# Linear attention with decay and a gated unit: features in natural order, a block-diagonal state per head pair, r transposed pair by pair, and another order of loads

## The chip, the cores and the metric

One core of one Trainium2 chip. The metric is the device time of one execution in microseconds; a kernel's time is the median of its runs. Runs that are over 1.5% slower than the fastest of the same kernel are called slow here; ratios are taken from the other, fast runs alone. The trace has a shorter time of its own, the span from the first to the last instruction, some 2 us below the run it was taken from. The engines are PE (matmuls), DVE (VectorE), ACT (ScalarE), POOL (GpSimd) and SP, which issues the transfers. All positions in a trace are microseconds from the span's start.

## The reference, cut to what matters

Two stages. First a linear attention with a decaying state for 4 batch entries (B), 8 heads (H), 768 positions (S) and 48 features a head (D); then a gated unit on the 384 joined features.

```python
for t in range(S):
    cur = u * k[t] (outer) v[t]
    y[t] = r[t] @ (state + cur)
    state = w[:, None] * state + k[t] (outer) v[t]
x = y joined over heads                       # [B, S, 384]
gate = sigmoid(causal convolution of x, 5 taps per feature)
out = (gate * (x @ w_val)) @ w_out
```

Of the kernel before, what the change touches and what calls it, by code (L numbers as in the profile page):

```python
# [16 lines left out]
def kernel(  # L17
# [12 lines left out]
    nc = tc.nc  # L30
# [13 lines left out]
    NG = J // 2  # L44
# [3 lines left out]
    ld = ctx.enter_context(tc.tile_pool(name="ld", bufs=4))  # L48
# [40 lines left out]
    load_r(0)  # L89
    load_kv(0, "v")  # L90

# [60 lines left out]
    rs_t = ring("rs", [128, 2, NP, 2, 64], 3)  # L152
    vb_t = ring("vb", [128, U, H * 64 + 64], 4)
    dv_t = ring("dv", [128, U, H * 64 + 64], 2)
    z_t = ring("z", [128, NP * 64 + 64], 6)
# [3 lines left out]
    for t_ in rs_t:  # L159
        nc.gpsimd.memset(t_[:, :, :, :, D:64].rearrange("p c n a x -> p (c n a) x"), 0.0)  # L160
    for t_ in vb_t + dv_t:
        nc.gpsimd.memset(gaps(t_.rearrange("p c x -> p (c x)")), 0.0)
    for t_ in z_t:
        nc.vector.memset(gaps(t_), 0.0)
# [5 lines left out]



# [5 lines left out]
    def load_weights():  # L178
        nc.sync.dma_start(out=cw5, in_=moe_conv_w)
        for dst, src in ((wv_st, moe_w_val), (wo_st, moe_w_out)):  # L180
            s5 = src.rearrange("(T s par e) n -> T s par e n", T=2, s=2, par=2)
            for s in range(2):
                for par in range(2):
                    q = 2 * s + par
                    nc.sync.dma_start(  # L185
                        out=dst[32 * q : 32 * q + 32, 0:2, :],
                        in_=s5[:, s, par, 16 * s : 16 * s + 32, :].transpose([1, 0, 2]),
                    )
                    e0 = 32 * (1 - s)
                    for T in range(2):  # L190
                        p0 = 32 * (2 * T + par) + 16 * s
                        nc.sync.dma_start(  # L192
                            out=dst[p0 : p0 + 16, 2, :], in_=s5[T, s, par, e0 : e0 + 16, :]
                        )

    wvA = consts.tile([128, NT, 2, 128], BF16)
    wvB = consts.tile([128, NT, 128], BF16)
    wout = consts.tile([128, NT, DM], BF16)
    cw5p = consts.tile([KW, NT, 128], BF16)
# [3 lines left out]
    def permute_cols(eng, dA, dB, src):  # L203

        s5 = src.rearrange("p g (s par e) -> p g s par e", s=2, par=2)
        a5 = dA.rearrange("p g (s par e) -> p g s par e", s=2, par=2)
        b5 = dB.rearrange("p g (par s e) -> p g par s e", s=2, par=2)
        for s in range(2):
            eng.tensor_copy(a5[:, :, s], s5[:, :, s, :, 16 * s : 16 * s + 32])
            e0 = 32 * (1 - s)  # L210
            eng.tensor_copy(b5[:, :, :, s], s5[:, :, s, :, e0 : e0 + 16])

    def prep_conv():
        permute_cols(
            nc.vector,
            cw5p[:, 0:2, :],
            cw5p[:, 2, :].rearrange("p (g x) -> p g x", g=2),
            cw5.rearrange("p (g x) -> p g x", g=2),
        )
        cw_ps = ps_mm.tile([128, NT, 8], BF16, name="mm_ps")  # L220
        for T in range(NT):
            nc.tensor.transpose(cw_ps[:, T, 0:KW], cw5p[:, T, :], ident[0:KW, 0:KW])
        nc.vector.tensor_copy(cwT, cw_ps[:, :, 0:KW])
# [9 lines left out]
    def prep_weights():  # L233
        permute_cols(
            nc.gpsimd,
            wvA.rearrange("p k T x -> p (k T) x"),
            wvB.rearrange("p k (T x) -> p (k T) x", T=2),
            wv_st.rearrange("p k (T x) -> p (k T) x", T=2),
        )

# [3 lines left out]
    def scale_r(b, g, eng):  # L244
        rs = rs_t[(b * NG + g) % 3]
        eng.tensor_tensor(  # L246
            out=rs[:, :, :, :, 0:D].rearrange("p j n a d -> p j (n a) d"),
            in0=r_st[b].rearrange("p h (j d) -> p j h d", d=D)[:, 2 * g : 2 * g + 2],
            in1=dr.rearrange("p h j d -> p j h d")[:, 2 * g : 2 * g + 2],
            op=ALU.mult,  # L250
        )

    def transp_r(b, g):
        if g == 0:
            st["rT", b] = wk.tile([128, NP, S], BF16, name="rT", bufs=3)
        rs = rs_t[(b * NG + g) % 3]
        tr = ps_tr.tile([128, 2, NP, 128], BF16, name="tr_ps")
        for j in range(2):
            for p in range(NP):
                nc.tensor.transpose(  # L260
                    tr[:, j, p, :], rs[:, j, p].rearrange("p a x -> p (a x)"), ident
                )
        nc.scalar.copy(  # L263
            out=st["rT", b].rearrange("x n (p j) -> x j n p", j=J)[:, 2 * g : 2 * g + 2],
            in_=tr,
        )
# [51 lines left out]
    def bonus_v(n):  # L318
        for cl in range(U):
            nc.gpsimd.tensor_tensor(  # L320
                out=heads(dv_t[n % 2][:, cl], H),
                in0=v_st[n][:, cl],
                in1=st["s", n][:, cl, :, None].to_broadcast([128, H, D]),
                op=ALU.mult,
            )
# [27 lines left out]
    nz = [0]  # L353

    def state(n, cl):
# [4 lines left out]
        kv_ps = ps_kv.tile([128, NP, D], F32, name="kv_ps")  # L360
        for p in range(NP):
            for par in range(2):
                h = 2 * p + par
                nc.tensor.matmul(
                    out=kv_ps[64 * par : 64 * par + 64, p, :],
                    lhsT=ks[:, cl, p, par, :],
                    rhs=heads(vb[:, cl], H)[:, h, :],
                    start=(p == 0),
                    stop=(p == NP - 1),
                    skip_group_check=True,  # L370
                )
        if c > 0:
            for par in range(2):
                nc.tensor.matmul(
                    out=kv_ps[64 * par : 64 * par + 64],
                    lhsT=ident[:, 64 * par : 64 * par + 64],
                    rhs=heads(st["z"], NP),
                    start=False,
                    stop=True,
                    skip_group_check=True,  # L380
                )
        st["kv_ps", n, cl] = kv_ps

    def decay(n, cl):
        c = (n % NU) * U + cl
        if c == NU * U - 1:
            return
        z = z_t[nz[0] % 6]
        nz[0] += 1
        nc.vector.tensor_tensor(  # L390
            out=heads(z, NP),
            in0=st["kv_ps", n, cl],
            in1=wct[:, :, None].to_broadcast([128, NP, D]),
            op=ALU.mult,
        )
# [4 lines left out]
    def y_out(n):  # L400
# [3 lines left out]
        ys = [ps_mm.tile([128, NT, 128], F32, name="mm_ps") for cl in range(U)]  # L404
        first = set()
        for kind, cl in (("z", 0), ("z", 1), ("a", 0), ("d", 0), ("a", 1), ("d", 1)):
            z = st.get(("zin", n, cl))
            if kind == "z" and z is None:
                continue
            for T2 in range(2):  # L410
                for h in range(H):
                    par, p = h % 2, h // 2
                    T = 2 if T2 else h // 4
                    q = (2 * (h // 4) + h % 2) if T2 else h % 4
                    rows = slice(64 * par, 64 * par + D)
                    s = p % 2
                    c0 = (48 if s == 0 else 0) if T2 else 16 + 16 * s
                    if kind == "z":
                        lt = z[rows, 64 * p + c0 : 64 * p + c0 + 32]
                        rh = rT[rows, p, cl * C : cl * C + C]  # L420
                    elif kind == "a":
                        lt = vb[:, cl, 64 * h + c0 : 64 * h + c0 + 32]
                        rh = st["at", n, cl][:, par, p, :]
                    else:
                        lt = dv[:, cl, 64 * h + c0 : 64 * h + c0 + 32]
                        rh = ident
                    nc.tensor.matmul(  # L427
                        out=ys[cl][32 * q : 32 * q + 32, T, :],
                        lhsT=lt,
                        rhs=rh,  # L430
                        start=(cl, q) not in first,
                        stop=(kind == "d" and T2 == 1),
                        skip_group_check=True,
                    )
                    first.add((cl, q))
            if kind == "d":
                t0 = PAD + cu * W + cl * C
                nc.scalar.copy(out=xT_t[b % 2][:, :, t0 : t0 + C], in_=ys[cl])  # L438
# [21 lines left out]
    def value(n):  # L460
# [3 lines left out]
        for Ts in ((0, 1), (2,)):  # L464
            v_ps = ps_mm.tile([128, len(Ts), W], F32, name="mm_ps")
            for i, T in enumerate(Ts):
                for kt in range(NT):
                    nc.tensor.matmul(  # L468
                        out=v_ps[:, i, :],
                        lhsT=wvA[:, kt, T, :] if T < 2 else wvB[:, kt, :],  # L470
# [35 lines left out]
    load_kv(1, "kv")  # L506
    load_weights()
    scale_k(0)
    scale_r(0, 0, nc.vector)
    scale_r(0, 1, nc.gpsimd)  # L510
    scale_r(0, 2, nc.vector)
    cast_v(0)
    for par in range(2):
# [3 lines left out]
        )  # L517

    for i in range(N + 3):
        x, a, y, f = i, i - 1, i - 2, i - 3  # L520
        if ok(x + 2):
            load_kv(x + 2, "kv")
        if x % NU == 0 and x // NU + 1 < B:
            load_r(x // NU + 1)
        if ok(a):
            prod(a)

        rb, rg = divmod(x + NU - 1, NG)
        if ok(x):
            transp_k(x)  # L530
        if x == 0:
            transp_r(0, 0)
            transp_r(0, 1)
            transp_r(0, 2)
# [67 lines left out]
```

## The kernel before: what the change and the argument touch

Both kernels take the positions in chunks of 128. Two chunks are a unit (256 positions of one batch entry), so there are 12 units. A loop of 15 passes is a software pipeline: pass i transposes k of unit i, forms the scores of unit i-1, the y of unit i-2, and the gated unit of unit i-3. Heads stand in PE tiles in pairs, each padded from 48 to 64 rows. In these traces PE takes its instructions in the order of the program: it stood idle for 8.4 us in front of the r transposes at 100.33 us, with output matmuls behind them whose input had been ready since 90.8. So the place of a step in the pass matters.

r of a whole batch entry (three units) is loaded, scaled and transposed into `rT`, one third per pass. Its positions are interleaved six to a partition (J = 6), so the copy from PSUM has to put position p*6+j in its place:

```python
def transp_r(b, g):
    ...                                       # 8 transposes: 2 values of j, 4 head pairs
    nc.scalar.copy(
        out=st["rT", b].rearrange("x n (p j) -> x j n p", j=J)[:, 2 * g : 2 * g + 2],
        in_=tr,                               # written bf16 elements are 12 bytes apart
    )
```

The order of the loop, cut:

```python
for i in range(N + 3):
    x, a, y, f = i, i - 1, i - 2, i - 3
    load_kv(x + 2, "kv")
    if x % NU == 0 and x // NU + 1 < B:
        load_r(x // NU + 1)                   # first used further down in this same pass
    prod(a); transp_k(x); conv(f); scale_k(x + 1)
    bonus(a); attn(a, 0); mask_at(a, 0); state(a, 0); decay(a, 0); bonus_v(a)
    scale_r(x // NU + 1, x % NU, nc.gpsimd)
    cast_v(x + 1); value(f)
    attn(a, 1); mask_at(a, 1); state(a, 1); decay(a, 1)
    y_out(y)
    transp_r(x // NU + 1, x % NU)             # PE stands here if r is late
    project(f)
    ...                                       # pass 0 also prepares the weights
```

Because y leaves PE in pieces of 32 features, the features of x stood in a permuted order; the weights were loaded in 24 small pieces to match.

## Time and profile before

| | before |
|---|---|
| median at the prediction, 3 runs | 169.73 us (168.91 to 170.16) |
| span of the trace | 165.8 us |
| busy: PE, DVE, ACT, POOL | 62, 47, 56, 35% |
| DMA | 20.57 MB, 50.6% of 16 engines' time in the main queue |

No engine is busy for two thirds of the span, so the averages say nothing yet. The page's row of 40 slices (each digit is the busy share of one slice in tenths, 9 meaning 90% or more) is what to read: it shows stages with different limits. The prediction below shows the lines.

### The profile page before, as it was taken

What the parts mean: (1) busy time and instruction counts of PE and PEld (TensorE: products, weight loads), DVE (VectorE), ACT (ScalarE), POOL (GpSimd) and SP (SyncE); (2) the same over time, 40 slices, a digit from 0 to 9 for tenths busy, and PEclk for the clock granted to TensorE, in tenths of its full rate; (3) what the DMA queues carried; (4) which work ended last, traced back from release to release, by engine and by line L of the source; (5) the groups of instructions that cost most, each with busy time, mean ns of one, the idle gap of its engine ahead of it and who ended that gap; (6) DMA issues with size and microseconds to landing.
All of it is one profiled execution on the core that took longest, in us unless ns stands there. A gap on an engine that the chain in (4) does not pass through costs nothing.

```text
span 165.8 us, 4872 instructions
## 1 busy us (share of the span) xinstructions
PE 103.5 (62%) x2123; PEld 81.6 (49%) x2123; DVE 77.2 (47%) x135; ACT 92.9 (56%) x109; POOL 58.9 (35%) x85
## 2 busy tenths in 40 slices
PE   0123100023579689596969108996969999999980
PEld 0112100022378568475747105775757878777750
DVE  0549000009898362391937500391947593953220
ACT  3979950009375928849394205849395817325441
POOL 7745000064877360370903024270906061230000
PEclk9999999999999978999999855899999999999999
DMA  4998338993187600390927940281927702020222
GB/s 74 269 247 187 104 105 169 301 229 73 24 170 167 218 4 0 94 195 6 248 45 182 241 151 0 88 166 38 241 47 174 182 31 99 4 97 12 91 95 95
DMA packets 58863, 20.57 MB, mean 124 GB/s; under 512 B 50773, under 2 KB 58842, under 8 KB 58842
## 3 DMA queue, kind: packets, MB, share of 16 engines
q1 hardware_dynamic: 58714, 20.26, 50.6%
q8 instruction: 16, 0.26, 0.7%
q14 instruction: 5, 0.04, 0.1%
q0 software_dynamic: 128, 0.00, 0.1%
HBM read 15.54 MB, written 4.72 MB: 122 GB/s over the span
## 4 chain that ended last, share of the span: by engine, by line
PE 44%; SPq 17%; ACT 10%; issue 9%; DMA 7%; POOL 5%; DVE 5%; DVEq 0%; ACTq 0%; POOLq 0%
PE mm_ps L427 11%; SPq L73 7%; DMA r_st<-in_r_dram 7%; PE mm_ps L448 7%; PE mm_ps L488 7%; PE mm_ps L468 6%; ACT o_sb L495 4%; PE tr_ps L260 4%; SPq L192 4%; ACT kT L290 4%; PE at_ps L334 3%; POOL rs L246 3%; PE tr_ps L287 3%; SPq L81 3%; SPq L185 2%
## 5 line engine op out<-in xcount | busy, mean ns | idle before, releaser
L263 ACT COPY rT<-tr_ps 128x1024 bf16<-128x1024 bf16 x12 | 42.7, 3620 | 29.2 <-PE tr_ps L260 29.0
L320 POOL TENSOR_TENSOR dv<-v_st,s_sb 128x384 bf16<-128x384 f32 x24 | 19.4, 830 | 57.1 <-PE at_ps L334 56.1
L260 PE MATMUL tr_ps<-ident,rs 128*128 128x128 bf16 x96 | 10.2, 272 | 34.1 <-POOL rs L246 28.9
L346 DVE TENSOR_TENSOR at<-at_ps,mask 128x1024 bf16<-128x1024 f32 x24 | 29.3, 1221 | 2.9 <-PE at_ps L334 1.9
L246 POOL TENSOR_TENSOR rs<-r_st,dr 128x768 bf16<-128x768 f32 x10 | 18.9, 1889 | 31.3 <-DMA r_st<-in_r_dram 31.3
L438 ACT CAST xT<-mm_ps 128x384 bf16<-128x384 f32 x24 | 11.2, 479 | 32.8 <-PE mm_ps L427 32.8
L448 PE MATMUL mm_ps<-xT,cwdiag 128*128 128x256 bf16 x180 | 22.8, 274 | 7.4 <-ACT o_sb L495 7.4
L260 PEld LDWEIGHTS <-rs 128*128 128x128 bf16 x96 | 7.8, 123 | 36.2 <-POOL rs L246 29.8
L448 PEld LDWEIGHTS <-cwdiag 128*128 128x128 bf16 x180 | 17.3, 98 | 10.7 <-issue 8.2
L316 DVE COPY s_sb<-mm_ps 128x16 f32<-128x16 f32 x12 | 2.1, 173 | 41.3 <-issue 34.5
L476 DVE TENSOR_TENSOR hT<-mm_ps,gate 128x512 bf16<-128x512 f32 (+1 forms) x24 | 12.2, 552 | 9.7 <-PE mm_ps L468 9.7
L488 PE MATMUL mm_ps<-wout,hT 128*128 128x384 bf16 x72 | 14.7, 344 | 0.5 <-DVE hT L476 0.5
L287 PE MATMUL tr_ps<-ident,ks 128*128 128x128 bf16 x96 | 9.1, 250 | 7.5 <-DVE ks L269 7.5
L495 ACT COPY o_sb<-mm_ps 128x384 f32<-128x384 f32 x24 | 12.2, 536 | 2.3 <-PE mm_ps L488 1.8
L279 POOL CAST vb<-v_st 128x384 bf16<-128x384 f32 x24 | 13.1, 576 | 0.0
L290 ACT COPY kT<-tr_ps 128x1024 bf16<-128x1024 bf16 x12 | 12.7, 1060 | 0.0
L269 DVE TENSOR_TENSOR ks<-k_st,dk 128x768 bf16<-128x768 f32 x12 | 12.0, 1002 | 1.2 <-DMA k_st<-in_k_dram 1.2
L468 PE MATMUL mm_ps<-xT,wvA 128*128 128x256 bf16 x72 | 9.8, 272 | 3.8 <-ACT gate L455 3.8
L455 ACT ACTIVATE gate<-mm_ps 128x512 bf16<-128x512 f32 (+1 forms) x24 | 10.8, 507 | 2.0 <-PE mm_ps L448 1.9
L287 PEld LDWEIGHTS <-ks 128*128 128x128 bf16 x96 | 7.6, 114 | 8.7 <-DVE ks L269 7.5
L334 PE MATMUL at_ps<-rT,kT 48*128 48x128 bf16 x192 | 10.4, 232 | 2.0 <-DVE at L346 1.9
L427 PE MATMUL mm_ps<-at,vb 128*32 128x128 bf16 x384 | 10.6, 235 | 0.0
(62 smaller groups left out, 137.1 us busy)
## 6 DMA issues: line engine op xcount, KB each, us to landing
k_st<-in_k_dram SPq DMA_DIRECT2D x24, 192.0 KB, 3.8
r_st<-in_r_dram SPq DMA_DIRECT2D x8, 576.0 KB, 5.8
v_st<-in_v_dram SPq DMA_DIRECT2D x24, 192.0 KB, 3.9
out_dram<-o_sb SPq DMA_DIRECT2D x12, 384.0 KB, 2.8
wv_st<-in_moe_w_val_dram SPq DMA_DIRECT2D x4, 96.0 KB, 2.1
wo_st<-in_moe_w_out_dram SPq DMA_DIRECT2D x4, 96.0 KB, 2.1
w_bc<-in_w_dram SPq DMA_DIRECT2D x1, 192.0 KB, 3.7
wv_st<-in_moe_w_val_dram SPq DMA_DIRECT2D x8, 24.0 KB, 1.9
```

Source lines behind the costliest of these rows:

```text
L246: eng.tensor_tensor(out=rs[:, :, :, :, 0:D].rearrange("p j n a d -> p j (n a) d"), in0=r_st[b].rearrange("p h (j d) -> p j h d", d=D)[:, 2 ...
L260: nc.tensor.transpose(tr[:, j, p, :], rs[:, j, p].rearrange("p a x -> p (a x)"), ident)
L263: nc.scalar.copy(out=st["rT", b].rearrange("x n (p j) -> x j n p", j=J)[:, 2 * g : 2 * g + 2], in_=tr,)
L287: nc.tensor.transpose(tr[:, cl, p, :], ks[:, cl, p].rearrange("p a x -> p (a x)"), ident)
L290: nc.scalar.copy(out=st["kT", n].rearrange("x n (c i) -> x c n i", c=U), in_=tr)
L320: nc.gpsimd.tensor_tensor(out=heads(dv_t[n % 2][:, cl], H), in0=v_st[n][:, cl], in1=st["s", n][:, cl, :, None].to_broadcast([128, H, D]), ...
L346: nc.vector.tensor_tensor(out=st["at", n, cl].rearrange("p a n i -> p (a n) i"), in0=st["at_ps", n, cl].rearrange("p a n i -> p (a n) i"), ...
L427: nc.tensor.matmul(out=ys[cl][32 * q : 32 * q + 32, T, :], lhsT=lt, rhs=rh, start=(cl, q) not in first, stop=(kind == "d" and T2 == 1), sk ...
L448: nc.tensor.matmul(out=g_ps[:, i, :], lhsT=cwdiag[:, T, t, :], rhs=xT[:, T, t0 + t : t0 + t + W], start=(t == 0), stop=(t == KW - 1),)
L468: nc.tensor.matmul(out=v_ps[:, i, :], lhsT=wvA[:, kt, T, :] if T < 2 else wvB[:, kt, :], rhs=xT[:, kt, t0 : t0 + W], start=(kt == 0), stop ...
L488: nc.tensor.matmul(out=o_ps, lhsT=hT[:, T, cl * C : cl * C + C], rhs=wout[:, T, :], start=(T == 0), stop=(T == NT - 1),)
L495: nc.scalar.copy(out=o_sb[:, cl, :], in_=o_ps)
```

## The change

Its intent is to take r out of the path and to do less shuffling. (1) r is scaled and transposed one head pair at a time over all six j, so the copy out of PSUM writes contiguous elements. (2) Loads: r of an entry is needed one to two passes after its load instead of in the same pass, k and v are loaded three units ahead instead of two. (3) y is made in the natural order of features, so weights load whole. For that the state of a head pair is one 128 by 96 block, and the zeros of `wcm` (the decay, as one factor per element) keep only its two diagonal blocks. (4) Some steps moved inside the pass: `conv` now comes before `transp_k`, `bonus_v` before `state`, `scale_k` and `cast_v` at the end. Core of the diff, much cut:

```diff
-    ld = ctx.enter_context(tc.tile_pool(name="ld", bufs=4))
+    ld = ctx.enter_context(tc.tile_pool(name="ld", bufs=5))
 ...
-        for dst, src in ((wv_st, moe_w_val), (wo_st, moe_w_out)):
-            ...                               (24 loads, permuted rows)
+        nc.sync.dma_start(out=wv_st, in_=moe_w_val.rearrange("(t p) n -> p t n", p=128))
+        nc.sync.dma_start(out=wo_st, in_=moe_w_out.rearrange("(t p) n -> p t n", p=128))
 ...
-            out=st["rT", b].rearrange("x n (p j) -> x j n p", j=J)[:, 2 * g : 2 * g + 2],
-            in_=tr,
+            out=st["rT", b][:, p, :].rearrange("x (p j) -> x p j", j=J),
+            in_=tr.rearrange("x j p -> x p j"),
 ...
-            for par in range(2):              (state: one head at a time, 64 columns)
-                nc.tensor.matmul(out=kv_ps[64 * par : 64 * par + 64, p, :], ...)
+            nc.tensor.matmul(out=kv_ps[:, p], ...)      (a pair, 128 columns, 96 wide)
 ...
-        for kind, cl in (("z", 0), ("z", 1), ("a", 0), ("d", 0), ("a", 1), ("d", 1)):
+        for cl in range(U):                   (12 state, 16 attention, 12 bonus matmuls;
+            ...                                before 16 of each)
 ...
-        if ok(x + 2):
-            load_kv(x + 2, "kv")
+        if ok(x + 3):
+            load_kv(x + 3, "kv")
 ...
+        rb, rp = {0: (x // NU, (2, 3)), 1: (0, ()), 2: (x // NU + 1, (0, 1))}[x % NU]
+            for p in rp:                      (after transp_k, before the scores)
+                transp_r(rb, p)
 ...
+        rb, rp = {1: (x // NU + 1, (0, 1)), 2: (x // NU + 1, (2, 3)), 0: (0, ())}[x % NU]
+            for p in rp:                      (at the end of the pass)
+                scale_r(rb, p, nc.gpsimd)
```

The weights are also prepared at the end of pass 1, no longer pass 0.

## The prediction

> **What bounds the kernel now.** I read the page's 40 slices first, then the groups, the chain that ended last in order of time, and the ACT timeline of one repeating unit. The kernel is a software pipeline over 12 units (256 positions of one batch entry): each pass of the loop transposes k of unit x, scores unit x-1, forms y of unit x-2, runs the gated unit on x-3. No engine is full over the span (PE 62%, ACT 56%), so I look for the stages. From the page's slices:
>
> ```profile
> PE   0123100023579689596969108996969999999980
> DMA  4998338993187600390927940281927702020222
> ```
>
> Three different limits show. Slices 5 to 9 (21 to 37 us) and 23 to 24: PE is empty. From slice 15 to 31 PE swings between 5 and 9. From slice 32 on PE is full. The chain explains the two empty stretches:
>
> ```profile
> 28.56 5.70 DMA r_st<-in_r_dram
> ...
> 34.43 1.81 POOL rs L246
> ...
> 36.29 1.03 PE tr_ps L260 x8
> ```
>
> ```profile
> 92.00 6.40 DMA r_st<-in_r_dram
> ...
> 98.47 1.81 POOL rs L246
> ...
> 100.33 1.03 PE tr_ps L260 x8
> ```
>
> Both are the same fault: r of the next batch entry is loaded and already scaled and transposed in the same pass, and PE, which works in order, stands behind it. In the first case the load is also late, because the 24 small weight issues hold the queue from 13.6 to 24.7 us: in the window 17 to 25 us the DMA engines were 41% busy at 109 GB/s, against 98% and 228 GB/s in 4 to 17 us. The swinging stretch is ACT:
>
> ```profile
> 72.68 0.93 ACT L438 CAST xT<-mm_ps 128x384 bf16<-128x384 f32 x2 [2.76 <-PE mm_ps L427]
> 73.65 3.59 ACT L263 COPY rT<-tr_ps 128x1024 bf16<-128x1024 bf16 x1
> 76.86 1.07 ACT L495 COPY o_sb<-mm_ps 128x384 f32<-128x384 f32 x2
> 77.81 1.03 ACT L290 COPY kT<-tr_ps 128x1024 bf16<-128x1024 bf16 x1
> 78.72 0.91 ACT L455 ACTIVATE gate<-mm_ps 128x512 bf16<-128x512 f32 x2
> ```
>
> The r copy out of PSUM takes 3.6 us, the k copy of the same size 1.03 us. The output copies and the gate queue behind it, PE waits for the gate, and a pass takes 9.5 to 9.8 us. Passes without it (the k transposes at 130.29 and 137.58 us) are 7.3 us apart with PE never idle in 130.45 to 144.8 us (14.35 us busy of 14.35).
>
> [...] The old r copy writes bf16 elements 12 bytes apart; 3620 against 1060 ns for 1024 elements agrees with a penalty on such writes. The new copy reads PSUM with 256 bytes between neighbours and writes contiguously. [...] no trace here shows an ACT read of this kind: this is the largest unknown. [...] The 96 y matmuls of a unit take 1.56 us, 16 ns each, so 32-column tiles do overlap here.
>
> **The change part by part.**
>
> (1) *Load order, and r one pass later.* r of batch entry 1 is now first needed at the end of pass 1, its transposes in pass 2; in every later entry the load has about two passes (some 15 us) ahead of it, against the 6.4 us it took in the chain. So the empty stretch at 92 to 100 us should go. At the start, the bytes ahead of the first half of r of entry 1 are w 0.20, k and v of units 0 to 2 2.36, r 1.18, weights 1.18, and 0.59 of its own: 5.5 MB. 0.3 MB had come by 4 us; at 228 GB/s the remaining 5.2 MB take 22.8 us. The weights (three issues now) and r come in larger packets; the page's slices with r in them reach 301 GB/s, so I take off 1.5 us: about 25.5 us. POOL then scales two pairs. A pair has 576 elements against 768: 1.81 x 576/768 = 1.36 us each, so 28.2 us, and pass 2 begins its scores at 28.6. POOL goes on with the v cast 0.96, the whole w_val cast (1152 elements; three times half of the 0.96 us for 2 x 384, 1.4), dv 1.62 and two more pairs 2.7: 35 us, and pass 3 begins its scores at about 35.7 us. Before, the same point (the second bonus matmuls after the ramp, pass 3) was at 55.73. **Gain 20 us.**
>
> (2) *r copy.* Now 16 copies of 768 elements for 12 of 1024. If a strided PSUM read costs nothing, interpolating the kT row (1024 elements, 1060 ns) and the xT row (384, 479 ns) gives 0.83 us each; 1.33 per pass, 1.1 us for 3.6. ACT then has 5.0 us a pass: kT 1.03, gate 0.9, xT 0.93, o_sb 1.07, r 1.1.
>
> (3) *State and y.* Per chunk: state 8 matmuls of 64 columns become 4 of 128 columns and N=96, about the same (0.24 us; 4 x 0.055 as for a 128-wide transpose); the carry becomes one of N=384, about 0.16 for 0.09. y falls from 96 to 80 a unit: z 32 to 24, now with all 128 rows, dv 32 to 24. At 14 ns each that saves 0.2 to 0.3 us. But in the second half of the attention part, neighbours in order now fall on the same 32 columns (1,1,0,0,3,3,2,2), so pairs go one after the other: 4 x 55 instead of 8 x 14 ns, +0.1 to 0.15 per chunk. Sum about zero: PE stays at 7.3 to 7.4 us, plus 12 transposes (0.66 us) in two passes of three.
>
> (4) *DVE.* The decay handles 384 instead of 192 elements: [...] 548 ns by the slope of its neighbours (the mask, 1024 elements, 1221 ns), twice a pass: DVE goes from about 6.0 to 6.4 us a pass. POOL keeps its 4.4.
>
> So a full pass is bound by PE at 7.4 us, 8.1 with transposes. In those, the second r transpose shares two PSUM buffers with k and must wait for the k copy, which comes behind the two gates on ACT: I add 0.4, 8.5 us. Passes 3 to 11: four at 7.5 and five at 8.5 are 72.5 us; I add 3 us for waits I don't see: 75.5, against 90.9 before (bonus 55.73 to 146.6). **Gain 15 us.** The tail from 146.6 to 165.8, 19.2 us, has neither loads nor r in it and stays. Span: 35.7 + 75.5 + 19.2 = 130.4; the median run stands 3.9 above the span before: **134 us.**
>
> **The rivals.** *The r copy stays slow, by its reads.*[...] At 3.3 ns each (the old rate) a copy is 2.7 us, 3.6 per pass on average, and the passes return to 9.3 where two copies fall: nine passes take some 83 us, time about 141. I give this three in ten. *DMA becomes the bound.* 1.57 MB a pass at 8 us is 196 GB/s, under the 218 to 228 seen when busy. That is near, and loads are gated by output transfers in the same queue; but with three units ahead a late load has slack. Time about 140 if it binds. *DVE in the loop.* 6.4 of 7.8 us with waits in series (mask, decay, product, mask) may stretch passes by 0.5 us: 138. *The startup is hidden anyway*, that is, something else (POOL behind the weights cast, cold matmuls) holds pass 3: each us late there is a us in full, as seen in the chain; I allow 4.
>
> **Range and chances.** Rivals push up by 4 to 8; a quicker ramp (r at 23 us), or DVE and ACT hidden wholly, pull down by 5. Range 126 to 143. Even with both main rivals the gain is 25 us, since the two empty stretches alone are worth more than 2%: faster 0.97, same 0.02, slower 0.01.
>
> **What would show it.** The r copy's mean (0.83 if right, 2.7 if the rival is); POOL's wait on r at the start near 25 us and no later one; k transposes 7.4 to 8.5 us apart in passes 3 to 11; PE near 75% of the span; the DMA share near 70% (20.57 MB at 228 GB/s are 90 us of 130). The prediction is wrong if r of entry 1 lands after 30 us, if passes stay above 9, or if the y matmuls grow past 2 us a unit.

The sum is 35.7 + 75.5 + 19.2 = 130.4, and 134.3 with the 3.9. The traces of the kernel before show this:

- The decay's 548 ns: the same line took 348 ns for 192 elements and the mask 1221 ns for 1024, so 1.05 ns an element and some 549 ns for 384.
- "Cold matmuls": eight r transposes took 0.82 us from start to next start after the empty stretch, at 100.33 us, and 0.45 at 110.44. The granted clock was 0.50 from 100.3 to 104 us and 1.00 from 108 to 112.
- "Larger packets": the page has 50773 of 58863 packets under 512 bytes; the program's rows of k and v, 192 bytes each, are 49152 of them. A row of r is 1152 bytes.
- "Gated by output transfers in the same queue": SP waited 83.3 us in 12 waits to issue the stores of o_sb, and the loads that follow in the program were issued right after (87.94 us after 87.44, 106.18 after 105.70, 115.87 after 115.40).
- That neighbours on the same 32 columns go one after the other, and that the r copy stays slow by its reads with a chance of three in ten, were estimates; no trace had shown either. e6 and e9 test them.

## The result, and the profile after

| | before | after |
|---|---|---|
| median, 4 runs each | 169.32 us (168.38 to 170.16) | 128.45 us (127.62 to 129.76) |
| span of the trace | 165.8 us | 126.4 us |
| busy: PE, DVE, ACT, POOL | 62, 47, 56, 35% | 77, 64, 52, 49% |
| mean DMA rate | 124 GB/s | 162 GB/s |

The ratio is 0.757 (95% interval 0.750 to 0.764). Here and below a ratio is the mean time of one kernel's fast runs over that of the kernel before's fast runs of the same rounds, so it isn't quite the ratio of the medians.

The same two rows of slices, of the changed kernel (a slice is now 3.16 us):

```profile
PE   0035853027987999979799997997999999999950
DMA  2999999899899979895599987903021030303123
```

One hole is left, slices 8 and 9 (22 to 28 us), and the stretch behind it is at 7 to 9 throughout. The DMA engines, idle in waves before, are now near full for most of the first 26 slices. The group of the r copy, before and after (line, engine, operation, output and input; then busy time, mean ns of one, and idle time before it):

```profile
L263 ACT COPY rT<-tr_ps 128x1024 bf16<-128x1024 bf16 x12 | 42.7, 3620 | 29.2 <-PE tr_ps L260 29.0
```

```profile
L222 ACT COPY rT<-tr_ps 128x768 bf16<-128x768 bf16 x16 | 12.3, 807 | 4.8 <-PE tr_ps L221 4.8
```

807 ns for 3620, and 12.3 us in all for 42.7. What is left of the late r is seen in the chain of work that ended last, followed back from the last instruction (start, length, what):

```profile
18.07 7.84 DMA r_st<-in_r_dram
...
26.05 2.76 POOL rs L209 x2
...
28.86 0.82 PE tr_ps L221 x6
```

The wait now ends 8 us earlier than before, one pass further on for POOL and two for PE, and there is no second one. To lay the times side by side I use the eight small matmuls by which each pass begins its scores ("bonus"). Before, those of pass 3 start at 55.73 us and of pass 12 at 146.32; after, at 39.30 and 108.33. (The prediction, and the first window below, took 146.6, where the next group of matmuls starts: 0.3 us too long.)

| stretch | before | after | gain |
|---|---|---|---|
| start to scores of pass 3 | 55.7 | 39.3 | 16.4 |
| passes 3 to 12 | 90.6 | 69.0 | 21.6 |
| rest | 19.5 | 18.1 | 1.4 |

The middle stretch, by the engines' busy times in that window, first before, then after (window, its length, busy microseconds and instructions of PE, weight loads, DVE, ACT, POOL; granted clock; DMA share and rate):

```profile
55.73:146.60 90.87, 71.36 (x1569) 56.61 (x1567) 48.54 (x76) 54.79 (x72) 32.48 (x40) 0.92 0.44 106
```

```profile
39.30:108.33 69.03, 65.47 (x1358) 52.16 (x1355) 51.93 (x77) 39.74 (x71) 37.43 (x42) 1.00 0.61 151
```

PE went from 79% to 95% of the stretch. Of the 21.6 us, 16 are PE's idle time (19.5 before, 3.6 after), 5.6 are less busy time. Only part of that is less work: e5 below has the matmuls of the kernel before without the long waits, and there they keep PE busy for 67.5 us of this stretch, against 71.1 in the kernel before and 65.5 in the changed one. So some 3.6 us of the busy time go with matmuls that ran slower after a wait (the eight r transposes, 0.82 us at 100.33 and 0.45 at 110.44), and 2.0 are saved by the new y and state.

### The profile page after: what moved, and what is told of

Its sections match the earlier page's. It is cut to its first block, busy times and chain, and to the rows that moved or that the text cites. A ratio compares the mean times of both kernels' runs of the same rounds, so it can differ in the third digit from the quotient of the medians.

```text
span 126.4 us, 4295 instructions
## 1 busy us (share of the span) xinstructions
PE 96.8 (77%) x1851; PEld 76.0 (60%) x1851; DVE 80.3 (64%) x130; ACT 66.0 (52%) x113; POOL 62.1 (49%) x84
## 3 DMA queue, kind: packets, MB, share of 16 engines
q1 hardware_dynamic: 58362, 20.26, 65.5%
## 4 chain that ended last, share of the span: by engine, by line
PE 63%; SPq 13%; DMA 6%; ACT 5%; DVE 5%; POOL 2%; issue 2%; DVEq 0%; POOLq 0%
PE mm_ps L397 16%; PE mm_ps L359 12%; PE mm_ps L437 10%; SPq L72 9%; PE mm_ps L417 7%; DMA r_st<-in_r_dram 6%; PE at_ps L293 5%; ACT kT L249 4%; PE kv_ps L319 3%; DVE at L305 3%; PE tr_ps L246 3%; PE tr_ps L221 3%; POOL rs L209 2%; SPq L80 2%; PE kv_ps L328 2%
## 5 line engine op out<-in xcount | busy, mean ns | idle before, releaser
L305 DVE TENSOR_TENSOR at<-at_ps,mask 128x1024 bf16<-128x1024 f32 x24 | 29.3, 1221 | 1.9 <-PE at_ps L293 0.8
L209 POOL TENSOR_TENSOR rs<-r_st,dr 128x576 bf16<-128x576 f32 x13 | 18.5, 1445 | 9.7 <-DMA r_st<-in_r_dram 9.7
L397 PE MATMUL mm_ps<-xT,cwdiag 128*128 128x256 bf16 x180 | 21.7, 272 | 0.6 <-ACT xT L387 0.6
L238 POOL CAST vb<-v_st 128x384 bf16<-128x384 f32 x24 | 18.1, 781 | 3.1 <-DMA v_st<-in_v_dram 3.1
L275 DVE COPY s_sb<-mm_ps 128x16 f32<-128x16 f32 x12 | 2.1, 175 | 25.1 <-issue 16.2
L222 ACT COPY rT<-tr_ps 128x768 bf16<-128x768 bf16 x16 | 12.3, 807 | 4.8 <-PE tr_ps L221 4.8
L437 PE MATMUL mm_ps<-wout,hT 128*128 128x384 bf16 x72 | 13.8, 328 | 0.5 <-DVE hT L425 0.5
L417 PE MATMUL mm_ps<-xT,wval 128*128 128x256 bf16 x108 | 13.8, 272 | 0.0
L228 DVE TENSOR_TENSOR ks<-k_st,dk 128x768 bf16<-128x768 f32 x12 | 12.6, 1053 | 0.8 <-DMA k_st<-in_k_dram 0.8
L444 ACT COPY o_sb<-mm_ps 128x384 f32<-128x384 f32 x24 | 11.5, 478 | 3.0 <-PE mm_ps L437 1.8
L249 ACT COPY kT<-tr_ps 128x1024 bf16<-128x1024 bf16 x12 | 12.1, 1011 | 1.0 <-PE tr_ps L246 0.4
L417 PEld LDWEIGHTS <-wval 128*128 128x128 bf16 x108 | 10.3, 97 | 1.5
```

What stands on the lines that cost most here:

```text
L209: eng.tensor_tensor(out=rs_t[p][:, :, :, 0:D].rearrange("p j a d -> p a j d"), in0=r_st[b][:, hs, :].rearrange("p a (j d) -> p a j d", d=D ...
L238: nc.gpsimd.tensor_copy(heads(vb[:, cl], H), v_st[n][:, cl])
L249: nc.scalar.copy(out=st["kT", n].rearrange("x n (c i) -> x c n i", c=U), in_=tr)
L305: nc.vector.tensor_tensor(out=st["at", n, cl].rearrange("p a n i -> p (a n) i"), in0=st["at_ps", n, cl].rearrange("p a n i -> p (a n) i"), ...
L397: nc.tensor.matmul(out=g_ps[:, i, :], lhsT=cwdiag[:, T, t, :], rhs=xT[:, T, t0 + t : t0 + t + W], start=(t == 0), stop=(t == KW - 1),)
L417: nc.tensor.matmul(out=v_ps[:, i, :], lhsT=wval[:, kt, T * 128 : T * 128 + 128], rhs=xT[:, kt, t0 : t0 + W], start=(kt == 0), stop=(kt == ...
```

## The experiments

Twelve kernels. Their results were all right. All ratios are to the kernel before in the same rounds; the changed kernel stands at 0.757.

**The r copy alone, undone (e1).** The theory: the 12-byte writes cost 3.6 us, and they lay on the path. The rival: ACT has slack, and only the loads counted. The edit turns the order of the copy and nothing else:

```diff
-            out=st["rT", b][:, p, :].rearrange("x (p j) -> x p j", j=J),
-            in_=tr.rearrange("x j p -> x p j"),
+            out=st["rT", b][:, p, :].rearrange("x (p j) -> x j p", j=J),
+            in_=tr,
```

> The changed kernel with one line turned: the r copy runs over the same elements in the other order, so it reads PSUM contiguously and writes bf16 elements 12 bytes apart, as the kernel before did. Theory (the strided write is what cost 3.6 us, and it sat in the pass): a copy goes from 0.81 to about 2.7 us (768 elements at 3.4 ns plus 0.1), ACT's transfers of y and the output come 1.5 to 2 us late in each pass with r transposes, about 136 us, that is 5 to 9% slower than the changed kernel's 128.5. Rival (ACT is 52% busy and has slack, the gain was the loads alone): copy 2.7 us, time within 2% of 128.5. Second rival (the order of the copy is not it; a copy of 768 elements is cheap anyway): copy stays near 0.8 us.

Measured: 137.08 us (136.64 to 138.29), ratio 0.819; 7% over the changed kernel by the medians. ACT's timeline in a pass with r, of e1:

```profile
58.37 1.01 ACT L249 COPY kT<-tr_ps 128x1024 bf16<-128x1024 bf16 x1
59.28 5.39 ACT L222 COPY rT<-tr_ps 128x768 bf16<-128x768 bf16 x2
64.27 1.10 ACT L387 CAST xT<-mm_ps 128x384 bf16<-128x384 f32 x2
```

and the same pass of the changed kernel:

```profile
53.50 1.01 ACT L249 COPY kT<-tr_ps 128x1024 bf16<-128x1024 bf16 x1
54.41 1.51 ACT L222 COPY rT<-tr_ps 128x768 bf16<-128x768 bf16 x2
58.40 1.04 ACT L387 CAST xT<-mm_ps 128x384 bf16<-128x384 f32 x2 [2.48 <-PE mm_ps L359]
```

Two copies take 5.4 instead of 1.5 us, and the copy of y (xT) follows without a gap where it had one of 2.5 us. So not all of the 3.9 us is lost, only what exceeds the slack. The rival falls, although ACT is busy for just 70% of e1: what counts is the place in the order. The passes are only half of it: of the 8.5 us by which e1's span is longer, 4.7 lie in passes 3 to 12, and 3.9 before them, where the four copies of the first r stand in a row for 10.4 us.

**The r copy alone, in the kernel before (e2).** With two values of j in a tile, at most two neighbours can be written together:

```diff
-            out=st["rT", b].rearrange("x n (p j) -> x j n p", j=J)[:, 2 * g : 2 * g + 2],
-            in_=tr,
+            out=st["rT", b].rearrange("x n (p j) -> x n p j", j=J)[:, :, :, 2 * g : 2 * g + 2],
+            in_=tr.rearrange("x j n p -> x n p j"),
```

> The kernel before with only the r copy's order turned as far as its two-block tiles allow: it writes two neighbouring bf16 elements, then steps 12 bytes, and reads PSUM with a stride of 1 KB for the inner two. Theory (cost per scattered write): half as many scattered writes, the copy goes from 3.62 to about 1.9 us, the passes that carry it from 9.5-9.8 to about 8 us, total about 160 us (6% faster). Rival (strided PSUM reads cost as much as strided writes): the copy stays at 3 us or more and the time is the same.

Measured: 154.4 us (ratio 0.920), more than either had it. The copy did not halve; it fell to 1.05 us, the time of a contiguous one (the k copy, 1.03 us; the group below, which is the same in e5). So two neighbours together, every 12 bytes, with a strided read of PSUM, cost next to nothing extra here: 1.05 against 1.03 us. That called for e9, below.

**The loads of r alone, in the kernel before (e3).**

```diff
     load_kv(1, "kv")
+    load_r(1)
     load_weights()
 ...
-        if x % NU == 0 and x // NU + 1 < B:
-            load_r(x // NU + 1)
+        if x % NU == 1 and x // NU + 2 < B:
+            load_r(x // NU + 2)
```

> The kernel before with only the loads of r moved: r of entry 1 ahead of the weights, r of each later entry two passes earlier. Theory (the two empty stretches are the late r, nothing else): PE's wait at 92-100 us goes (about 8 us, with the cold matmuls after it 9), and the first wait ends near 22 us instead of 36 (12 us or more), total about 148 us. Rival (k, v or the slow r copies take the place of the wait): under half of that, 160 us or more.

Measured: 153.18 us (ratio 0.907): between the two. Beyond the start no wait for r is left, but the gain at the start is partly given back. The profile of e3 fell in a slow run, so I take the times from e5 below, which has the same loads and a fast profile: scores of pass 1 start at 28.6 us instead of 41.3, those of pass 2 at 39.7 instead of 47.4. k of unit 2 now stands behind r and the 24 weight loads in the queue, and DVE waits 4.9 us for it. A wait took the place of the one removed.

**Both in the kernel before (e5).** The edits of e2 and e3 together.

> The kernel before with both of the last call's changes: the r copy writing two neighbours at a time, and the loads of r moved early. Apart they saved 13.5 and 14.8 us of 167.9. Theory (they are different stretches of time, and what e3 fell short by was the slow r copies filling the gap): at least additive, 136 to 140 us, that leaves 8 to 11 us of the change's gain to the weights in three loads, the loads further ahead and the natural order. Rival (both wait for the same thing): under additive, 145 us or more.

Measured: 137.82 us, ratio 0.821. Apart they take 8.0 and 9.3 points off the ratio, together 17.9: they add up, as parts of different stretches do. The row of the r copy in e5:

```profile
L263 ACT COPY rT<-tr_ps 128x1024 bf16<-128x1024 bf16 x12 | 12.5, 1049 | 17.1 <-PE tr_ps L260 16.9
```

About three quarters of the change's gain (17.9 of 24.3 points) is had without the natural order, the new state or the third unit. And in e5's trace the three stretches of the table above are 49.2, 68.5 and 19.5 us: passes 3 to 12 are already as short as the changed kernel's 69.0. What e5 lacks lies in the start (9.9 us) and the rest (1.4).

**The weights in 24 pieces, in the changed kernel (e4).**

```diff
-        nc.sync.dma_start(out=wv_st, in_=moe_w_val.rearrange("(t p) n -> p t n", p=128))
-        nc.sync.dma_start(out=wo_st, in_=moe_w_out.rearrange("(t p) n -> p t n", p=128))
+        for dst, src in ((wv_st, moe_w_val), (wo_st, moe_w_out)):
+            for t in range(NT):
+                for q in range(4):
+                    nc.sync.dma_start(
+                        out=dst[32 * q : 32 * q + 32, t, :],
+                        in_=src[128 * t + 32 * q : 128 * t + 32 * q + 32, :],
+                    )
```

> The changed kernel with the two weight matrices loaded in 24 pieces of 32 rows, in the same place of the queue and with the same bytes. Theory (issue time of 24 small loads holds the queue): 24 x 0.47 us = 11 us of issue for 0.9, DMA near 105 GB/s in that stretch, r of entry 1 lands 5 to 7 us later than 25.9 us, and the whole kernel is 5 to 7 us longer, about 134.5. Rival (the queue has enough in flight, the issues are hidden): within 1 us of 128.5.

Measured: 135.14 us, ratio 0.805; 6.7 us over the changed kernel by the medians. The queue of e4 and then of the changed kernel (start, length of issue):

```profile
14.98 5.42 SPq L181 DMA_DIRECT2D wv_st<-in_moe_w_val_dram  x12
20.44 5.52 SPq L181 DMA_DIRECT2D wo_st<-in_moe_w_out_dram  x12
26.01 1.05 SPq L72 DMA_DIRECT2D v_st<-in_v_dram  x2
27.10 1.18 SPq L80 DMA_DIRECT2D r_st<-in_r_dram  x2
```

```profile
15.89 0.38 SPq L178 DMA_DIRECT2D wv_st<-in_moe_w_val_dram  x1
16.32 0.48 SPq L179 DMA_DIRECT2D wo_st<-in_moe_w_out_dram  x1
16.85 1.18 SPq L72 DMA_DIRECT2D v_st<-in_v_dram  x2
18.07 4.60 SPq L80 DMA_DIRECT2D r_st<-in_r_dram  x2
```

The 24 issues of 48 KB took 10.9 us, 0.46 us each. From 14 to 28 us the DMA engines moved 133 GB/s at a share of 0.56 in e4, 262 GB/s at 1.00 in the changed kernel. r's issue is the chain's link in both: it landed at 31.8 us in e4 and at 25.9 in the changed kernel, 5.9 us apart. So the whole weights matter, not for their transfer but for what queues behind their issue.

**The order of the attention matmuls of y (e6).** The prediction held that neighbours on the same 32 output partitions run one after the other.

```diff
-                for h in range(H):
+                for h in ((0, 2, 4, 6, 1, 3, 5, 7) if x else range(H)):
```

> The changed kernel with the second half of the attention matmuls of y taken in the order of heads 0,2,4,6,1,3,5,7, so that no two neighbours write the same 32 output partitions (the prediction reckoned that the pairs 1,1,0,0,3,3,2,2 run one after the other). If that step of the prediction holds: the 16 attention matmuls of a chunk start over 0.22 us now because of it and shrink, 0.1 to 0.15 us a chunk, 2.4 to 3.6 us in all, ratio to before near 0.74. Rival (neighbours on the same partitions cost nothing, as 0.22 us for 16 matmuls in both kernels suggests): the 16 keep 0.22 us and the ratio stays at 0.757.

Measured: 127.65 us, ratio 0.760 (0.756 to 0.764): the same. The 16 matmuls are 0.22 us from the next part in both kernels, so no cost of neighbours on the same partitions is seen. The step was wrong, see below.

**Two units ahead (e7).**

```diff
-    ld = ctx.enter_context(tc.tile_pool(name="ld", bufs=5))
+    ld = ctx.enter_context(tc.tile_pool(name="ld", bufs=4))
 ...
-        if ok(x + 3):
-            load_kv(x + 3, "kv")
+        if x > 0 and ok(x + 2):
+            load_kv(x + 2, "kv")
```

> The changed kernel with k and v loaded two units ahead instead of three (four buffers instead of five), all else as it is. Theory (a load has nearly two passes, 14 us, and lands in 4.5 to 10 us, so three units are not needed): within 1% of 128.5, no new wait on k or v. Rival (the queue is full in the first 95 us and the third unit is what hides it): waits of DVE and POOL on k and v in several passes, 132 us or more.

Measured: 127.84 us, ratio 0.760 (0.754 to 0.766): the same, with no new wait on k or v in the passes. The third unit and its buffers buy nothing here. (The first three units are still loaded at the start in this kernel; it is the loop's distance alone that was tested.)

**r ahead of the weights, in the changed kernel (e8).**

```diff
+    load_kv(1, "v")
     load_kv(2, "k")
-    load_kv(1, "v")
+    load_r(1)
 ...
+    load_kv(2, "v")
     load_weights()
-    load_kv(2, "v")
 ...                                       (pass 0 no longer loads r)
-        if i == 1:
+        if i == 2:
             prep_conv()
```

> The changed kernel with r of entry 1 loaded ahead of the weights and of v of unit 2, and the preparation of the weights one pass later so that nothing waits for them in order. Theory (the ramp is set by the landing of the first half of r of entry 1): 1.57 MB fewer ahead of it, at 262 GB/s 6 us earlier, POOL's first scaling of entry 1 near 20 us instead of 26.05, scores of pass 3 near 34 instead of 39.3, total 123 to 125. Rival (the bytes bound the ramp whatever their order, or cold matmuls do): pass 3 no earlier, 128 us.

Measured: 127.94 us, ratio 0.761: no gain, a miss. Scores of pass 2 did come at 25.0 instead of 29.5 us. But pass 3's came at 39.1 instead of 39.3. The chain of e8 shows what ate it:

```profile
23.27 6.49 DMA k_st<-in_k_dram
29.85 1.01 DVE ks L229
30.86 0.58 DVE cw5b L189
...
31.97 3.56 DVE cwdiag L198 x3
35.57 1.25 PE mm_ps L398 x5
```

k of unit 3 is now the late load, and the making of the convolution's diagonal matrices (cwdiag), which I had moved from pass 1, where it lay in the wait, to the end of pass 2, now stands before the convolution. From the cast of the small weights (cw5b) to the last matrix that is 4.6 us of the chain. My experiment had put a new wait in place of the old one; as a test of the theory it is inconclusive.

**What a scattered write costs, measured by itself (e9).** After the end of the changed kernel, sixteen copies of 512 bf16 elements per partition, all but one from one PSUM tile, for instance:

```diff
+    nc.scalar.copy(out=single(8), in_=h5)     # every 8th element, 16 bytes apart
+    nc.scalar.copy(out=pair(16), in_=h2)      # two neighbours, then 32 bytes on
```

> The changed kernel with sixteen copies out of one PSUM tile of 512 bf16 elements added after its end (their results are thrown away; the output is right): ACT writing every 1st, 2nd, 4th, 8th, 16th bf16 element, pairs of neighbours 8, 16 and 32 bytes apart, fp32 elements together and 24 bytes apart, one with a strided PSUM read, one with a strided SBUF read, and four on DVE. Theory[...]: steps 2 and 4 cost no more than contiguous (0.55 us), steps 8 and 16 cost 1.8 us, pairs are free up to 16 bytes and at 32. Rival (a lone 2-byte write costs three to four element times wherever the next one is): every single step from 2 on takes about 1.8 us, all pairs and both fp32 forms 0.55. Both expect 0.55 for the strided read.

Measured (one look), ACT's timeline. L540 to L544: bf16 elements 2, 4, 8, 16 and 32 bytes apart. L545 to L547: pairs of neighbours every 8, 16, 32 bytes. L548 and L549: fp32, together and 24 bytes apart. L550: strided PSUM read. L551: strided SBUF read, 32 bytes apart.

```profile
122.58 0.59 ACT L540 COPY scr<-tr_ps 128x512 bf16<-128x512 bf16 x1
123.19 0.73 ACT L541 COPY scr<-tr_ps 128x512 bf16<-128x512 bf16 x1
123.95 1.29 ACT L542 COPY scr<-tr_ps 128x512 bf16<-128x512 bf16 x1
125.27 2.42 ACT L543 COPY scr<-tr_ps 128x512 bf16<-128x512 bf16 x1
127.72 2.29 ACT L544 COPY scr<-tr_ps 128x512 bf16<-128x512 bf16 x1
130.05 0.58 ACT L545 COPY scr<-tr_ps 128x512 bf16<-128x512 bf16 x1
130.66 0.61 ACT L546 COPY scr<-tr_ps 128x512 bf16<-128x512 bf16 x1
131.30 0.62 ACT L547 COPY scr<-tr_ps 128x512 bf16<-128x512 bf16 x1
131.81 0.59 ACT L548 CAST scf<-tr_ps 128x512 f32<-128x512 bf16 x1
132.43 1.05 ACT L549 CAST scf<-tr_ps 128x512 f32<-128x512 bf16 x1
133.27 0.63 ACT L550 COPY scr<-tr_ps 128x512 bf16<-128x512 bf16 x1
133.93 1.11 ACT L551 COPY scr<-scr 128x512 bf16<-128x512 bf16 x1
```

Neither expectation holds. Single 2-byte writes got dearer with their distance up to 16 bytes and no further (0.59 us together; 0.73, 1.29 and 2.42 at 4, 8 and 16 bytes; 2.29 at 32). Take 0.16 us off each for the fixed part (an estimate, chosen to fit) and divide by the 16-byte stretches touched, 16 bytes being the distance from which on it got no dearer: 0.57 us over 128 stretches, 1.13 over 256, 2.26 and 2.13 over 512, that is 4.2 to 4.5 ns a stretch every time. Elements 12 bytes apart touch 0.75 stretches each, so 3.3 ns an element, and 1024 of them 3.4 + 0.16 = 3.5 us: the 3.62 of the copy before. But one pair alone in every second stretch costs hardly more than contiguous writes (0.62 against 0.59), and lone fp32 words 24 bytes apart cost (1.05 - 0.16)/512 = 1.7 ns. So in these copies it is the lone 2-byte write that is dear, not the stretch. DVE, at 0.42 us contiguous, gave 0.72 at 4 bytes, 2.29 at 32, 0.62 for pairs 32 bytes apart: the same for lone writes, while its pairs did cost more than contiguous ones. The strided PSUM read, 256 bytes between neighbours, cost ACT 0.63 against 0.59, nothing to speak of; the SBUF read, 32 bytes apart, 1.11. Why a lone half word costs this, no run here shows.

**PE kept warm (e10).** How much of the ramp is matmuls that run slower after the wait? In the changed kernel eight attention matmuls took 0.61 us in pass 2 and 0.40 in pass 3, the granted clock was 0.53 from 28 to 36 us and 1.00 from 36 to 40; "cold" and "warm" below stand for that. Sixteen matmuls whose result is thrown away were put into the wait:

```diff
+        if i == 2:
+            wm = ps_kv.tile([128, 384], F32, name="kv_ps")
+            for q in range(16):
+                nc.tensor.matmul(out=wm, lhsT=ident, rhs=rs_t[3]...[:, 0:384],
+                                 start=(q == 0), stop=(q == 15))
+            nc.vector.tensor_copy(wm_sb, wm)
```

> The changed kernel with 16 idle matmuls of 384 columns put into PE's wait for r in pass 2 (21 to 27 us), so that pass 2 starts with a warm clock. Theory (pass 2 to 3 took 9.8 us instead of the 7.1 predicted because its chain of scores, masks and y runs in order, not because PE is cold): the y part and transposes shorten by some 1.5 us together, total 127 to 128.5. Rival (the cold clock is the cause): scores of pass 3 come 2.5 us or more earlier, near 36.5 us, total 126 or less.

Measured: fast runs 125.26 to 125.98 us, ratio 0.750 (0.745 to 0.755), whose interval touches that of the changed kernel. The trace: scores of pass 2 at 28.39 us and of pass 3 at 36.67, 8.3 us apart, against 9.8 in the changed kernel and 10.2 to 10.4 in the traces of e6, e7 and e9, which have nearly the same ramp. The first attention matmuls of pass 2, in the changed kernel and in e10:

```profile
29.80 0.61 PE L293 MATMUL at_ps<-rT,kT 48*128 48x128 bf16 x8
```

```profile
28.66 0.40 PE L294 MATMUL at_ps<-rT,kT 48*128 48x128 bf16 x8
```

So the slower matmuls cost 1.5 to 2.1 us there. (They are read from their lengths, not from the clock records: over the whole run those give 0.924 for the changed kernel and 0.994 for e6, though in both the first eight attention matmuls of pass 2 took 0.61 us and those of pass 3 0.40.) The rest of the 2.6 us by which pass 3 is earlier comes mostly from r, whose scaling on POOL began 1 us earlier in this trace (25.1 us; without the warming, 25.2 in e6 and 26.2 in e7). The outcome lies between the two expectations: 8.3 us remain with the first eight at 0.40 us, so the order of PE's chain is the main part of the stretch, as the theory had it; but pass 3 at 36.67 and the total under 126 are the rival's figures. Of the 2.7 us by which this pass outlasted the predicted 7.1, the slower matmuls are 1.5, the larger part.

**A version meant to beat both (e11).** e8's lesson used: r of entry 1, v of unit 2 and k of unit 3 ahead of the weights, the small convolution weights first of all, only the two large casts moved to pass 2; and the second r transpose of a pass behind its first scores.

```diff
     nc.sync.dma_start(out=w_bc, in_=w.partition_broadcast(128))
+    nc.sync.dma_start(out=cw5, in_=moe_conv_w)
 ...
+    load_kv(1, "v")
     load_kv(2, "k")
-    load_kv(1, "v")
+    load_r(1)
+    load_kv(2, "v")
+    load_kv(3, "k")
 ...                                       (the loop's loads and the two casts to match)
-            for p in rp:
+            for p in rp[:1] if x > 0 else rp:
                 transp_r(rb, p)
 ...
+        if x > 0 and rb < B:                  (behind the scores, before value(f))
+            for p in rp[1:]:
+                transp_r(rb, p)
```

> A version meant to beat the changed kernel: r of entry 1, v of unit 2 and k of unit 3 ahead of the weights; the small conv weights first of all, so that their preparation stays in pass 1 (in e8 it moved onto the path), the two large casts a pass later; and the second r transpose of a pass after its first scores, so that it needs no wait for the k copy. Theory (the ramp is set by the landing of r of entry 1 and k of unit 3; each of four passes loses 0.77 us at that wait): pass 3's scores near 35.5 instead of 39.3, the r passes 8.0 instead of 8.7 us, total about 122. Rival (the bytes bound the ramp and PE the passes): 126 or more.

Measured: 120.86 us (120.04 to 121.81), ratio 0.721. Scores of pass 3 at 35.9 us, passes with r 7.5 to 8.1 instead of 8.7 us: the theory held. The wait that the split takes away is this one, of the changed kernel (its bracket: idle time and what ended it):

```profile
54.57 0.49 PE L221 MATMUL tr_ps<-ident,rs 128*128 128x128 bf16 x6 [0.77 <-ACT kT L249]
```

In e11 DVE made the diagonal matrices from 21.1 to 26.6 us, ahead of the product that the scores of pass 2 need.

**The diagonal matrices on ACT (e12).** ACT had nothing to do at that time.

```diff
-        nc.vector.tensor_tensor(out=cwdiag[:, T], in0=ident..., in1=cwT..., op=ALU.mult)
+        for t in range(KW):
+            nc.scalar.activation(out=cwdiag[:, T, t, :], in_=ident,
+                                 func=AF.Identity, scale=cwT[:, T, t : t + 1])
 ...
-        if i == 1:
+        if i == 0:
             prep_conv()
```

> e11 with the diagonal tap matrices of the convolution made by ACT (15 scaled copies of the identity) in its idle stretch of pass 1, and their small transposes in pass 0, for in e11 VectorE made them from 21.1 to 26.6 us, beside POOL's scaling, ahead of the product that pass 2's scores wait for. Theory (that is now the end of the wait in the ramp, r being ready at 24 us): scores of pass 2 at 24.5 instead of 27.4, pass 3 at 33 instead of 35.9, total about 118. Rival (k of unit 3 or the byte count holds pass 3): pass 2 earlier, pass 3 and the total unchanged, 120.5.

Measured: 117.52 us (117.12 to 118.32), ratio 0.705 (0.701 to 0.709): 30% under the kernel before and 7% under the changed kernel. Scores of pass 2 at 23.6 us, of pass 3 at 32.3. The window from pass 3 to pass 12 of e12:

```profile
32.33:97.67 65.34, 64.79 (x1364) 52.12 (x1362) 52.92 (x77) 41.10 (x72) 37.77 (x43) 1.00 0.72 177
```

PE is busy for 99% of it (a busy PE, as the trace counts it, need not be at its fastest: the same eight attention matmuls counted as 0.61 us busy in pass 2 of the changed kernel and as 0.40 in pass 3). Removing waits can take hardly more from these passes; what is left to try is less or denser PE work.

## Why the prediction was right or wrong

Predicted 134 us, range 126 to 143; measured 128.45. The mechanism was right in its large parts; sizes and two steps were off. That the sum came within 6 us owes something to luck: the ramp was 3.6 us longer than predicted, the rest 9.5 us shorter.

*The r copy* was put at 0.83 us if strided PSUM reads are free: 807 ns. Its rival (slow by its reads, three in ten) did not come; e9 shows the read cost by itself, 0.63 us against 0.59. That the copy lay on the path is shown by e1 and e2.

*The second empty stretch* was to go: POOL's waits for r are two, 9.7 us in all, the longest the one that ends at 26 us.

*The first r* was put at 25.5 us and scores of pass 2 at 28.6: r landed at 25.9, scores at 29.5. e4 confirms the weights' part in it.

*Pass 3 at 35.7 us* was wrong: 39.3. 0.9 us of it is the later start of pass 2. The step that failed is "two more pairs 2.7: 35 us, and pass 3 begins its scores at about 35.7 us". It followed POOL alone. POOL was indeed done at 35.1, but PE's own chain of pass 2 was longer than the 7.1 us left for it: scores, a mask on DVE, scores, y, its copy, the convolution, the k transposes and their copy, 9.8 us from scores to scores. The chain of the changed kernel:

```profile
31.73 0.61 PE at_ps L293 x8
...
33.10 1.97 PE mm_ps L359 x67
...
35.09 0.49 ACT xT L387
...
35.61 1.80 PE mm_ps L397 x15
...
37.90 1.02 ACT kT L249
```

1.5 us or somewhat more of it are the slower matmuls after the wait (e10), and 1.2 us above the 7.1 remain without them. The prediction had "cold matmuls" among its rivals and allowed 4 us there: that rival came true in part. Gain 16.4 instead of 20.

*The passes* were put at 75.5 us and took 69.0. Four things make up the 6.5. The 3 us "for waits I don't see" were not needed. "Four at 7.5 and five at 8.5" was a wrong count: between the scores of pass 3 and of pass 12 lie the transposes of passes 5, 6, 8 and 9, four, so 1 us less. The four took 8.7, with the wait of 0.77 us where I had added 0.4: 0.8 us more. And five plain ones took 6.8 on average instead of 7.5: 3.3 us less. The 7.5 counted all five as passes of the fullest kind; but passes 3, 6 and 9 form one state fewer (6.80 us each), and from pass 11 to 12 no k is transposed (6.60 us, and 6.65 already in the kernel before). The shorter y is the smaller part. "+0.1 to 0.15 per chunk" for neighbours on the same columns was the second step that failed, and with it "Sum about zero": the 16 attention matmuls take 0.22 us in either order (e6), the state and bonus parts shrank to 0.18 and 0.16 us, and y of a unit takes 1.24 to 1.38 us for 1.57. Yet pass 10, full in both kernels, took 7.29 us before and 7.20 after.

*DVE and DMA* did not become the bound: DVE 51.9 us of the middle 69.0, DMA share 0.61. That loads are three units ahead was of no use (e7).

*The tail* was 18.1 us for 19.2 (19.5 from the right mark), and the median stands 2.0 above the span instead of 3.9: the 3.9 set the median beside the span of a faster run; every run of the changed kernel stands 1.8 above its own. The ramp's +3.6, the passes' -6.5, the tail's -1.1 and this -1.9 give the 5.9 us between 134.3, the unrounded sum, and 128.45.

What each part is worth: the copy and the loads of r together three quarters of the gain (e5, shown in the kernel before), the whole weights 6.7 us (e4, shown in the changed kernel). What is left is 9.4 us by the medians of e5 and the changed kernel less 6.7, some 3 us. The shorter y in the passes is not it: e5 has the old y and state, and its passes 3 to 12 are no longer (68.5 against 69.0 us). The new y and state saved PE 2.0 us there, and the four waits of 0.77 us for the k copy, which came with the new order of the transposes, cost 3.1. By the traces the rest of the kernel, which has no such wait, is 1.4 us shorter than in e5, and the start by 9.9, of which the whole weights are 6.0 (scores of pass 3 at 45.35 in e4, 39.30 in the changed kernel). The other 4 us of the start lie among the order of the k and v loads, r needed a pass or two later, the weights prepared a pass later and the steps moved inside the pass; no run undid any of these, nor the natural order or the block-diagonal state, alone, so these shares are not shown.

## What to carry to other kernels

Ask of each load not how long it takes but in which pass its first user stands, and what stands behind that user on its engine (here PE stood idle for 8.4 us); and count the issues ahead of it in the queue as well as the bytes (here 24 of 0.46 us). An engine that is half idle can still set the pace if its one slow instruction lies ahead of copies that others wait for (here ACT, busy 56%, with a copy of 3.62 us). When a step is moved out of a wait, look where it lands: in e8 it put 4.6 us into the chain, and e12 won 3 by giving the matrices to the engine that was idle. And compare stretch by stretch, not the totals alone: the new y and state save PE work in every pass, and the wait that came with the change gave it back until e11 took it away.
